# Attention and mixture of experts in one kernel: routing links moved apart, q and k loaded in halves, gathers dealt out one by one, and both ends of the attention re-ordered

## The chip, the core and the metric

The kernel runs on one core of a Trainium2 chip. The metric is the device time of one execution in microseconds (us). Five engines work side by side, each through its own queue in order: TensorE (PE; its weight loads are listed as PEld), VectorE (DVE), ScalarE (ACT), GpSimd (POOL) and SyncE (SP), which here only issues DMAs. ScalarE and GpSimd issue some DMAs too. SBUF is the working memory, PSUM the memory into which TensorE writes.

## The reference

Eight batches of eight heads, 576 tokens, head size 64. q and k are rotated (rotary embedding), attention follows, and its output is the input of a layer of eight experts, in which each token goes to one expert:

```python
q_rot, k_rot = rotate(q), rotate(k)              # [8, 8, 576, 64]
attn = softmax(q_rot @ k_rot^T / sqrt(64))
x = (attn @ v) as [4608 tokens, 512]
logits = x @ w_gate + modality_bias[modality_id]  # 8 experts
e = argmax(logits);  g = softmax(logits)[e]
out[token] = g * (relu(x @ w1[e]) @ w2[e])        # 512 -> 1024 -> 512
```

All in float32. The kernel reaches that precision in the products of scores and experts by splitting each operand into a high and a low half (H, L) and summing three products.

## The kernel before, in words

**Attention.** The 64 heads are 32 pairs (`NPAIR`), four to a batch. A pair's q and k come as one tile of two halves, `R[:, 0]` and `R[:, 1]` (the second is the first with its halves of the head size swapped, so that a rotation is a*cos + b*sin). `rope_` (L224) has five parts: 0 multiplies a by COS (L230), 1 multiplies b by SIN (L232), 2 adds them (L234), 3 copies the high half on ScalarE (L236, the helper's line L221), 4 subtracts to get the low half (L238). In the order below parts 0 to 4 are called T1, T2, R, HI, LO. For pairs 0 and 1 VectorE does parts 0, 1, 2 and 4, for all others GpSimd. Two buffers `R` live in the staging areas ST1 and ST2 of the expert weights, COS behind the one, SIN behind the other. `swap` (L240) copies the halves to the other 64 partitions by DMA, into `SW`. `load` (L138) brings q and k, `loadv` (L142) brings V in four DMAs.

Scores are made in nine units S0 to S8 (L250, matmuls L261) in a ring of three PSUM tiles. `rowmin` (MN, VectorE, L270) and `expo` (EX, ScalarE, L277) turn a unit into P; then `fill` (F0 to F3, FA, FB, L283) transposes P on TensorE, and ScalarE (A_) and VectorE (B_) evict the transposes into PH and PD. `AV` (AVA, AVB, L339) multiplies by V in two parts, `avout` (OT) copies to oT, `outp` (OUTA, OUTB, L370; the last rows in L373) turns the result with RW, an identity beside the gate's weights, so that x and its logits come in one product; `ev` (EVA, EVB, L384 to L390) scales by the reciprocal sums into X, into G (logits) and into XT (the last 64 tokens). `xout` (XO) stores a batch of X to DRAM in five DMAs.

**Order.** Nothing is scheduled by need: `J` (L700) gives each of these steps a key, a step of pair n stands at its key in `KEYS` plus n x 14.438 (`PER`), and all are issued in the order of keys (L819). The engines go through their queues in that order. So the keys, which are in the unit of microseconds of the plan, say what stands behind what; they start nothing at a time. `AT` holds the keys of routing and experts.

**Routing.** After the last pair of a batch `route` (L405) computes the token's expert and its rank among the expert's tokens, in 13 links that go from engine to engine (`rk` in `AT`): reductions on VectorE, comparisons on GpSimd, exponentials on ScalarE, one product on TensorE (L450, L452). They stand from 0 to 15.2 behind the pair's EVA, in the next pair. `scatter` (L469) writes five times to a table TAB in DRAM, by indirect DMA of GpSimd, one every 9 us of the plan. TAB holds, expert by expert, the token and its weight.

**Experts.** The tokens of an expert are taken in blocks of 256. `plan` (L479) computes the blocks: a first plan of `NA` = 8 whole blocks from the batches 0 to 5 (28 links from pair 23 on, on GpSimd and VectorE, 1.5 apart; among them a shift, L492), and a second one of up to 17 from all tokens, of which 11 are unrolled and six more stand in a guarded loop (L895), which runs when the second plan has over 11. A block: `m_ix` (L601) loads indices from TAB on SP's queue, `m_gather` (L608, L614) fetches rows of X into XG by eight indirect DMAs, `m_tr`/`m_tre` (L653, L657) transpose and split them, `m_l1` (L663, L673) is the first layer, `m_l1e` (L677) its relu and split, `m_l2` (L684, L690) the second layer, scaled into y (L693) and scattered to the output (L694). Weights come by `m_load1` and `m_load2` (L624, L629; left out where the expert stays), and `m_hi`, `m_lo` split them (L218, L221). Block 0 is placed by hand among the last pairs (L789 to L818): its plan and weights, gathers, splits and its first layer, whose four parts stand between AVB and OUTA of pair 31; the gathers of blocks 0, 1 and 2 are issued by turns. The attention's buffers are then released as a whole (L824), the two planes of W2 and y are allocated in their place, and a loop (`chain`, L845) goes on with the blocks. The last batch's routing, its scatters and the second plan are put between its steps.

**Start.** `setup` (L170) clears buffers and loads constants by DMAs of GpSimd; pair 0 is loaded and rotated in three chunks of columns (`FIRST`, L151), then pair 1 whole; `setup2` (L202) computes the modality's part of the logits and two constants, on GpSimd. The units of pair 0 stand in the order of all pairs, S8 first, which needs the last chunk.

Of the kernel before, what the change touches and what calls it, by code (L numbers as in the profile page):

```python
# [8 lines left out]
F32 = mybir.dt.float32  # L9
# [9 lines left out]
P = 128  # L19
# [6 lines left out]
NB_STATIC = 11  # L26
EMPTY = 1 << 20
# [17 lines left out]
    rk=(0, 0.6, 1.5, 4.7, 5.5, 6.3, 6.9, 7.5, 9.6, 10.4, 11.2, 14.4, 15.2),  # L45
    pl=1.5,
    sc=(10.5, 9.0),
    tr=3.5,
    te=-8.0,
    hi=(-14.0, -9.0, -5.0, -1.0),  # L50
    l1=(7.0, 10.0, 13.7, 17.6),
    l1e=3.0,
    sp2=(0.2, 0.4, 1.4, 1.8),
    l2=2.0,
    w1=(1.0, 5.7, 8.0, 10.2),
    w2=(-8.0, -5.0, -2.0, 1.0),
    plan=(-99.0, -15.0, 4.0, 6.0, 8.0, 10.0, 12.0, 14.0),
    ix=(-16.5, -9.5, 4.0, 6.0),
    rows=4.0,
    gap=1.3,  # L60
# [5 lines left out]
def tile_attention_moe(ctx: ExitStack, tc: tile.TileContext, qk, v, mod, wg, mb, w1, w2, rope, cf, ci, out):  # L66
# [42 lines left out]
    pp = att.enter_context(tc.tile_pool(name="pp", bufs=1))  # L109
# [4 lines left out]
    PJ = [pp.tile([P, 2 * S], F32, name=f"P{j}") for j in range(4)]  # L114
    P4 = pp.tile([P, S + 128], F32, name="P4")
    PH = pp.tile([P, 8, S], F32, name="PH")
    PD = pp.tile([P, S], F32, name="PD")
    Vs = [pp.tile([P, 2, 5, 64], F32, name=f"V{i}") for i in range(2)]

    RW = pp.tile([P, 4, 2, 72], F32, name="RW")  # L120

# [16 lines left out]
    def load(n):  # L138
        nc.sync.dma_start(out=Rs[n % 2], in_=qk[n])
        st[n] = dict(R=Rs[n % 2], HL=HL[n % 2], SW=SW[n % 2], V=Vs[n % 2])  # L140

    def loadv(n):  # L142
        b, hp = divmod(n, 4)
        V = Vs[n % 2]
        for hh in range(2):
            src = v[b, 2 * hp + hh]
            nc.sync.dma_start(out=V[:, hh, 0:4, :], in_=src[0:512, :].rearrange("(p j) d -> p j d", j=4))
            nc.sync.dma_start(out=V[hh * 64:hh * 64 + 64, hh, 4, :], in_=src[512:576, :])

# [7 lines left out]
    load(1)  # L157
# [10 lines left out]
    G = rc.tile([P, 5, 9, E], F32, name="G")  # L168

    def setup():  # L170
# [10 lines left out]
        for h in range(4):  # L181
            for s in range(2):
                g.tensor_copy(RW[s * 64:s * 64 + 64, h, s, 0:64], idf[s * 64:s * 64 + 64, s * 64:s * 64 + 64])
        g.memset(MI, 0)
        TI = PH.rearrange("p a b -> p (a b)")[:, 0:(E + 1) * N * 2 // P].bitcast(I32)
# [5 lines left out]
        for s in range(2):  # L191
            g.dma_start(out=RW[s * 64:s * 64 + 64, :, s, 64:72], in_=wg.rearrange("(c s d) e -> s d c e", s=2, d=64)[s])
        g.dma_start(out=CF, in_=cf)
        g.dma_start(out=VAL, in_=ci)
        m32 = mod.bitcast(I32).rearrange("(b s w) -> b s w", s=S, w=2)
        g.dma_start(out=MI[:, :, 0:4, :], in_=m32[:, 0:512, :].rearrange("b (p j) w -> p b j w", j=4))
        g.dma_start(out=MI[0:64, :, 4, :], in_=m32[:, 512:576, :].rearrange("b p w -> p b w"))
        for i in range(2):
            g.dma_start(out=MBB[:, i, :], in_=mb[i:i + 1, :].to_broadcast([P, E]))
        g.dma_start(out=TAB.rearrange("(p r) w -> p (r w)", p=P), in_=TI)  # L200

    def setup2():  # L202
        g = nc.gpsimd
        BT = PJ[0][:, 0:B * 5 * E].rearrange("p (b e) -> p b e", e=E)
        g.tensor_copy(MF, MI[:, :, :, 0])
        sh = [P, B * 5, E]
        mf = MF.rearrange("p b j -> p (b j)").unsqueeze(2).to_broadcast(sh)
        bi = BI.rearrange("p b j e -> p (b j) e")
        g.tensor_tensor(bi, mf, MBB[:, 1:2, :].to_broadcast(sh), op=ALU.mult)
        g.tensor_scalar(MF, MF, -1.0, 1.0, op0=ALU.mult, op1=ALU.add)  # L210
        g.tensor_tensor(BT, mf, MBB[:, 0:1, :].to_broadcast(sh), op=ALU.mult)
        g.tensor_tensor(bi, bi, BT, op=ALU.add)
        g.tensor_copy(UT, cview("U"))
        g.tensor_copy(RUN[:, 0, :], cview("EB"))
# [9 lines left out]
    def rope_(n, part, c0=0, c1=QW):  # L224
        d = st[n]
        e = nc.vector if n < 2 else nc.gpsimd
# [105 lines left out]
    def AV(n, half):  # L332
# [3 lines left out]
        for kt in range(5):  # L336
            for hh in range(2):
                r = PH[:, 4 * hh + kt, c0:c1] if kt < 4 else PD[:, c0:c1]
                nc.tensor.matmul(pa[hh * 64:hh * 64 + 64, 0:c1 - c0], d["V"][:, hh, kt, :], r, start=(kt == 0), stop=(kt == 4))  # L339
# [19 lines left out]
    def outp(n, half):  # L359
# [3 lines left out]
        if b not in bt_:  # L363
            bt_[b] = dict(x=xo.tile([P, 4, DM], F32, name="X", tag="X"), xt=xo.tile([P, 4, 72], F32, name="XT", tag="XT"))
        po = d["po", half] = psA.tile([P, 512], F32, name="pa", tag="pa")
        w = RW[:, hp].rearrange("p s c -> p (s c)")
        for i in range(2):
            for s in range(2):
                c = (2 * half + i) * P + s * 64
                nc.tensor.matmul(po[s * 64:s * 64 + 64, i * 144:i * 144 + 144], oT[:, c:c + 64], w, start=True, stop=True)  # L370
# [4 lines left out]
    def ev(n, half):  # L375
# [8 lines left out]
        nc.vector.tensor_tensor(xv, pv[:, :, 0:64].rearrange("p a (i f) -> p a i f", f=32),  # L384
                                rv.unsqueeze(2).unsqueeze(3).to_broadcast([P, 4, 2, 32]), op=ALU.mult)
        gv = G[:, j0:j0 + 2, 2 * hp:2 * hp + 2, :]
        nc.vector.tensor_tensor(gv, pv[:, :, 64:72].rearrange("p (j s) e -> p j s e", s=2),
                                rv.rearrange("p (j s) -> p j s", s=2).unsqueeze(3).to_broadcast([P, 2, 2, 8]), op=ALU.mult)
        if half:
            nc.vector.tensor_scalar(Bt["xt"][:, hp, :], po[:, 288:360], ri[:, 8:9], None, op0=ALU.mult)  # L390

    def xout(b):
# [3 lines left out]
        xt = xd[512:576, :].rearrange("p (i c f) -> p i c f", c=4, f=32)  # L396
        for i in range(4):
            s, o = i // 2 * 64, i % 2 * 32
            nc.sync.dma_start(out=xt[:, i], in_=Bt["xt"][s:s + 64, :, o:o + 32])
# [5 lines left out]
    def route(b):  # L405
        Bt = bt_[b]
        V_ = nc.vector
        G_ = nc.gpsimd
# [5 lines left out]
        for s in range(2):  # L414
# [583 lines left out]
```

## Time and profile before

| | |
|---|---|
| median of 3 runs | 983.05 us (978.0 to 984.02) |
| the profiled execution: its time, its span | 978.22 us, 976.4 us |
| TensorE busy | 908.2 us, 93% |
| VectorE, ScalarE, GpSimd busy | 674.2, 632.3, 663.8 us |
| mean granted TensorE clock | 0.982 |
| moved by DMA | 132.71 MB, mean 136 GB/s |

The profile is of one execution. The span goes from the first to the last instruction on the chip; the time holds what lies around it too. A line of the timeline gives start, duration, engine, line of the kernel, operation, what is written from what, and in brackets how long the engine stood idle before and who ended that. A line of the groups gives count, busy us and mean ns, then the idle time before and its causes. A line of the waits gives who waited for whom, us in total, how often, and the longest.

### The profile page before, as it was taken

Reading aid. Unit: us, or ns where it says so; the run is one execution under the profiler, and the core shown is the slowest. Engines: PE = TensorE matmul, PEld = TensorE weight load, DVE = VectorE, ACT = ScalarE, POOL = GpSimd, SP = SyncE. Lnnn points to the kernel's source line nnn. Section 1 sums busy time; section 2 is a strip of 40 time slices with the busy share of each in tenths; the row PEclk is TensorE's granted clock in tenths of the full one; section 3 lists DMA queues with packets and bytes.
Section 4 is the critical chain, followed back from the end, with each engine's and each line's share of the span. In section 5 each row is a group of like instructions: output and inputs, shape, how many; then the busy total and the mean of one; then the engine's idle time right before and its main releaser. Section 6 shows DMA issues by size and latency. Waiting matters only on the chain. (4 is left out here: it accounts for less than half of the span.)

```text
span 976.4 us, 24969 instructions
## 1 busy us (share of the span) xinstructions
PE 908.2 (93%) x9248; PEld 742.4 (76%) x9248; DVE 674.2 (69%) x1158; ACT 632.3 (65%) x1299; POOL 663.8 (68%) x498
## 2 busy tenths in 40 slices
PE   1899999999999999989977899999999999999996
PEld 1677677777777767767646689999998888899995
DVE  6677777787777777777754478677666666666771
ACT  1778787787787877868753355666555656556661
POOL 7776788889878798799656076557666666556500
PEclk9799999999999999999989899999999999999998
DMA  9645667566574755746751261111431611611100
GB/s 285 194 142 173 180 198 221 148 188 202 174 225 134 201 185 175 228 130 182 207 149 34 64 211 36 55 48 58 142 120 42 218 38 45 227 44 49 41 24 15
DMA packets 71964, 132.71 MB, mean 136 GB/s; under 512 B 28395, under 2 KB 48267, under 8 KB 66844
## 3 DMA queue, kind: packets, MB, share of 16 engines
q1 hardware_dynamic: 61436, 110.32, 37.8%
q0 software_dynamic: 9536, 19.48, 6.4%
q8 instruction: 75, 1.23, 0.6%
q10 hardware_dynamic: 864, 1.25, 0.4%
q14 instruction: 53, 0.43, 0.2%
HBM read 140.59 MB, written 19.77 MB: 164 GB/s over the span
## 5 line engine op out<-in xcount | busy, mean ns | idle before, releaser
L270 DVE TENSOR_REDUCE mn<-ps 128x1 f32<-128x576 f32 x288 | 205.4, 744 | 104.2 <-PE ps L261 67.3
L277 ACT ACTIVATE P<-ps,mn 128x576 f32<-128x576 f32 x288 | 210.4, 737 | 97.6 <-DVE mn L270 90.4
L614 POOL DMA_INDIRECT XG<-X,iy x152 | 180.9, 1190 | 47.5 <-issue 41.4
L673 PE MATMUL psH<-HL,W1H 128*128 128x256 f32 x1152 | 202.7, 279 | 0.0
L261 PE MATMUL ps<-HL 64*128 64x288 f32 x960 | 170.7, 315 | 29.8 <-ACT HL L221 14.9
L261 PE MATMUL ps<-SW 64*128 64x288 f32 x960 | 170.3, 316 | 9.0 <-DMA SW<-HL 4.7
L261 PEld LDWEIGHTS ps<-HL 64*128 64x128 f32 x960 | 137.7, 190 | 53.2 <-ACT P L277 15.9
L673 PEld LDWEIGHTS psH<-HL,W1H 128*128 128x128 f32 x1152 | 176.8, 188 | 1.7
L673 PE MATMUL psH<-HL,W1L 128*128 128x256 f32 x576 | 160.8, 279 | 0.7 <-DVE W1L L218 0.7
L261 PEld LDWEIGHTS ps<-SW 64*128 64x128 f32 x960 | 135.4, 190 | 24.4 <-ACT P L277 14.1
L218 DVE TENSOR_TENSOR W1L<-ST,W1H 128x1024 fp32r<-128x1024 f32 x76 | 90.0, 1222 | 84.6 <-ACT W1H L221 82.6
L339 PE MATMUL pa<-PH,V 128*64 128x320 f32 (+1 forms) x1024 | 142.2, 420 | 1.1 <-PE ps L261 0.7
L694 POOL DMA_INDIRECT out_dram<-y,ix x38 | 39.1, 1030 | 143.6 <-ACT y L693 129.8
L690 PE MATMUL psY<-W2H,SW 128*128 128x512 f32 x304 | 120.3, 396 | 1.4 <-ACT W2H L221 1.4
L690 PE MATMUL psY<-W2L,SW 128*128 128x512 f32 x304 | 120.4, 396 | 0.4 <-DVE W2L L218 0.4
L283 PE MATMUL ps<-idf,P 64*128 64x64 f32 x2624 | 105.3, 229 | 8.8 <-DVE PH L315 2.4
L283 PEld LDWEIGHTS ps<-idf,P 64*128 64x128 f32 x2624 | 92.6, 141 | 22.7 <-ACT PH L221 8.6
L315 DVE COPY PH<-ps 128x512 f32<-128x512 f32 (+1 forms) x160 | 97.3, 632 | 17.4 <-PE ps L283 10.9
L339 PEld LDWEIGHTS pa<-PH,V 128*64 128x64 f32 x1024 | 69.8, 139 | 51.5 <-issue 14.5
L673 PEld LDWEIGHTS psH<-HL,W1L 128*128 128x128 f32 x576 | 108.2, 188 | 0.9 <-DVE W1L L218 0.9
L221 ACT ACTIVATE PH<-ps 128x512 f32<-128x512 f32 (+1 forms) x160 | 84.0, 556 | 22.1 <-PE ps L283 14.9
L218 DVE TENSOR_TENSOR W2L<-ST,W2H 128x1024 fp32r<-128x1024 f32 x76 | 92.4, 1220 | 4.1 <-ACT W2H L221 3.6
(159 smaller groups left out, 1602.9 us busy)
## 6 DMA issues: line engine op xcount, KB each, us to landing
ST<-in_moe_w_dram SPq DMA_DIRECT2D x152, 512.0 KB
ST<-in_qk_dram SPq DMA_DIRECT2D x31, 1216.0 KB
SW<-HL SPq DMA_DIRECT2D x124, 232.0 KB
V<-in_v_dram SPq DMA_DIRECT2D x64, 128.0 KB
X<-X SPq DMA_DIRECT2D x8, 1024.0 KB
XG<-X,iy POOLq DMA_INDIRECT x152
V<-in_v_dram SPq DMA_DIRECT2D x64, 16.0 KB
X<-XT SPq DMA_DIRECT2D x32, 32.0 KB
```

The source lines that it names most:

```text
L218: nc.vector.tensor_tensor(o, a, b, op=ALU.subtract)
L221: return nc.scalar.activation(o, i, AF.Copy, scale=scale)
L261: free(nc.tensor.matmul(ps[:, g, 0:288], t[:, wq, q0:q0 + P], t[:, wk, k0:k0 + 288], start=(m == 0), stop=(m == len(L) - 1)), seen)
L270: lastmin[d["ring", u]] = nc.vector.tensor_reduce(mn, d["S", u][:, :, 0:288], op=ALU.min, axis=AX.XY).ins
L277: nc.scalar.activation(p.rearrange("p (a b) -> p a b", a=2), ps[:, :, 0:288], AF.Exp, bias=d.pop(("m", u)), scale=-1.0, accum_out=d["sum"] ...
L283: free(nc.tensor.transpose(ps[0][:, g, c:c + 64], src[r, k0:k0 + P], idf[r, r]), ps[1])
L315: mine.append((nc.vector.tensor_copy if g else acopy)(o, i).ins)
L339: nc.tensor.matmul(pa[hh * 64:hh * 64 + 64, 0:c1 - c0], d["V"][:, hh, kt, :], r, start=(kt == 0), stop=(kt == 4))
L614: nc.gpsimd.indirect_dma_start(out=XG[s % 2][:, t, g, :], out_offset=None, in_=X.rearrange("n (i f) -> (n i) f", f=P)[0:rows], in_offset=b ...
L673: nc.tensor.matmul(ps[:, i, :], w[:, c, f0:f0 + P], x[:, c, :], start=(m == 0), stop=(m == 11))
L690: nc.tensor.matmul(ps, hx[:, c, t * P:(t + 1) * P], w[:, c, :], start=(m == 0), stop=(m == 23))
L694: nc.gpsimd.indirect_dma_start(out=out, out_offset=bass.IndirectOffsetOnAxis(ap=d["ix"][:, t, 0:1], axis=0), in_=y, in_offset=None, bounds ...
```

## The change

- **Routing.** 15 links for 13 (the first copy goes to GpSimd as a step of its own, some are re-ordered), at keys from 23.0 to 73.3 behind the batch's last pair, so over three and a half pairs. Scatters stand one a pair from 73.4 on. In the last batch GpSimd's part goes to VectorE.
- **First plan.** It covers five batches (`NPL`), not six, begins after pair 19, has nine links (`plan0`), without the shift and the casts; whole blocks are counted by comparing with multiples of 256. Scatters of other batches are declared independent of each other, and those of batches 5 to 7 of block 0 to 7's index loads.
- **Loads.** `load` takes a half; b comes first, long ahead (key -48.9), a at -39.33 as before; b x SIN (now at T1) is done before a x COS. V comes in three DMAs, XT goes out in two, from two buffers; the gate's columns lie 4 by 4 behind 32 of x.
- **Gathers.** Each of the gathers of blocks 0, 1, 2 has a key, some wait for a named matmul (AV or OUT of pair 30, the first layer of block 0).
- **Start.** Pair 0's units get keys of their own (`first`), S1 and S0 ahead; pair 1 is rotated by GpSimd, but for its LO; constants are loaded by ScalarE's queue; `setup2` goes to VectorE in two parts, at 12.9 and 17.3 of pair 0.
- **End.** Pair 31 has keys of its own (`last`), both AV halves at once after the fills, then block 0's first layer, with the output products in it. W2's planes lie in the places of P and of PH, released one by one (`weights2`); W2 is split among the first layer's steps. y has its own pool from the start.

Core of the diff:

```diff
-    rk=(0, 0.6, 1.5, 4.7, 5.5, 6.3, 6.9, 7.5, 9.6, 10.4, 11.2, 14.4, 15.2),
-    pl=1.5,
-    sc=(10.5, 9.0),
...
+    rk=(23.0, 28.55, 31.2, 36.9, 41.45, 43.0, 44.4, 45.7, 54.6, 56.9, 57.4, 58.85, 60.2, 70.35, 73.3),
+    sc=(73.4, 87.85, 102.3, 116.7, 116.75),
+    pl=(58.9, 70.4, 73.35, 84.85, 87.75, 99.3, 102.2, 113.7, 116.6),
+    ix=(-41.5, -3.9, 6.1, 9.1),
+    sine=-48.9,
+    rows=(((0, -27.5, None), (1, -13.05, None), (2, -12.4, None), (3, -2.9, (30, "av", 0)), (5, 0.45, (30, "av", 1)),
+           (7, 4.75, (30, "out", 1))), ((0, 11.15, ("l1", 0)),), ((0, 16.5, None),)),
+    hi=(-14.8, -14.7, -0.4, -0.3),
+    lo=(-11.8, -1.6, 10.8, 10.85),
+    tr=(10.2, 10.21),
+    te=(10.3, 10.4),
+    hi2=(10.5, 10.98, 11.1, 11.2),
+    lo2=(11.5, 11.55, 11.65, 11.75),
+    last=dict(AVA=10.3, AVB=10.4, RE=10.2, RI=10.25, OTA=10.96, OTB=11.0, OUTB=11.2, OUTA=11.21, ...),
+    l1=(11.1, 11.3, 11.4, 11.42),
+    first=dict(S1=-5.9, S0=-5.85, MN1=-5.8, MN0=-5.75, EX1=-5.7, EX0=-5.65, S6=-5.55, S7=-5.5, ...),
+    second=dict(HI=-20.04, LO=-19.79),
+    consts=(12.9, 17.3),
...
-    def load(n):
-        nc.sync.dma_start(out=Rs[n % 2], in_=qk[n])
+    def load(n, half):
+        nc.sync.dma_start(out=Rs[n % 2][:, half], in_=qk[n, :, half])
...
-        e = nc.vector if n < 2 else nc.gpsimd
+        e = nc.vector if n == 0 or (n, part) == (1, 4) else nc.gpsimd
...
+    def weights2(i):
+        places[i].close()
+        W2[i] = ctx.enter_context(tc.tile_pool(name=f"w2{i}", bufs=1, reuse_waits="tile", ...)).tile(
+            [P, 8, DM], F32R, name="W2" + "HL"[i])
...
-    def setup2():
-        g = nc.gpsimd
+    def setup2(part):
+        g = nc.vector
...
+    def plan0():
+        G_ = nc.gpsimd
...
+        most = NPL * S // BLK
+        G_.tensor_tensor(nf, RUN[0:1, NPL, :], cview("EB")[0:1], op=ALU.subtract)
+        G_.tensor_scalar(th, sl[:, 0:most], float(BLK), float(BLK), op0=ALU.mult, op1=ALU.add)
+        G_.tensor_tensor(full, nf.unsqueeze(2).to_broadcast(sh), th.unsqueeze(1).to_broadcast(sh), op=ALU.subtract)
+        G_.tensor_scalar(full, full, 0.0, None, op0=ALU.is_ge)
+        yield
+        total(nb, full)
...
+        if after is not None:
+            tc.add_manual_dep(inst.ins, (l1_[after[1]] if after[0] == "l1" else st[after[0]][after[1:]]).name, ...)
...
-        if n > 1:
-            for part, nm in enumerate(("T1", "T2", "R", "HI", "LO")):
+        if n > 0:
+            for part, nm in ((1, "T1"), (0, "T2"), (2, "R"), (3, "HI"), (4, "LO")):
                 K_(nm, rope_, n, part)
...
-        if n > 3:
-            K_("LD", load, n)
+        if n > 2:
+            J(AT["sine3" if n == 3 else "sine"], "LD", n, load, n, 1)
+            K_("LD", load, n, 0)
```

422 lines of the change are left out of this document (246 added, 176 removed).

## The prediction, made before the changed kernel ran

> **What bounds the kernel now.** I read the page first, then TensorE's idle gaps in the timeline, and with them cut the span into five stretches and asked for the busy time of each.
>
> ```profile
> span 976.4 us, 24969 instructions
> PE 908.2 (93%) x9248; PEld 742.4 (76%) x9248; DVE 674.2 (69%) x1158; ACT 632.3 (65%) x1299; POOL 663.8 (68%) x498
> ```
> ```profile
> 14.86:47.24 32.38, 24.34 (x251) 18.90 (x252) 22.80 (x32) 18.20 (x45) 25.98 (x14) 0.84 0.68 213
> 47.24:473.64 426.40, 408.32 (x5697) 306.21 (x5695) 318.95 (x701) 329.21 (x869) 354.98 (x221) 1.00 0.62 182
> 473.64:563.99 90.35, 72.06 (x714) 53.56 (x711) 50.25 (x94) 45.43 (x97) 40.17 (x41) 0.91 0.38 104
> 563.99:967.58 403.59, 403.50 (x2596) 363.76 (x2596) 274.18 (x315) 235.87 (x286) 230.11 (x193) 1.00 0.26 85
> 967.58:976.40 8.82, 0.00 (x0) 0.00 (x0) 0.00 (x0) 0.69 (x1) 0.97 (x1) 0.70 0.06 21
> ```
>
> Columns of the second view: stretch, length, busy us (and instructions) of PE, PEld, DVE, ACT, POOL, granted clock, DMA share, GB/s. TensorE is the bound: 908.2 of 976.4 us. The cuts are events on it. 14.86 is the first score matmul. 47.24 and 473.64 are the second output projection (L373) of pair 0 and of pair 28; 563.99 is where TensorE has block 1 of the experts before it, 967.58 the last output.
>
> ```profile
> 14.86 0.60 PE L261 MATMUL ps<-HL 64*128 64x288 f32 x1 [14.86 <-ACT HL L221]
> ...
> 18.42 0.60 PE L261 MATMUL ps<-SW 64*128 64x288 f32 x1 [2.96 <-DMA SW<-HL]
> ...
> 32.08 4.13 PE L283 MATMUL ps<-idf,P 64*128 64x64 f32 x71 [0.44 <-ACT P L277]
> ...
> 47.24 0.29 PE L373 MATMUL pa<-RW,oT 128*64 128x72 f32 x4
> ...
> 473.64 0.29 PE L373 MATMUL pa<-RW,oT 128*64 128x72 f32 x4
> ```
>
> The experts' stretch is TensorE alone (403.50 of 403.59 us). Two outputs one block apart give its pace:
>
> ```profile
> 945.18 0.69 ACT L693 ACTIVATE y<-psY,ix 128x512 f32<-128x512 f32 x1 [3.02 <-issue]
> ...
> 967.58 0.69 ACT L693 ACTIVATE y<-psY,ix 128x512 f32<-128x512 f32 x1 [4.91 <-PE psY L690]
> ```
>
> That is 22.40 us a block, and 18 blocks are 403.2. Nothing in the change touches these matmuls, so 403.6 and the 8.8 of the tail stay. What can move is ahead of 563.99. For its floor I take a pair undisturbed by routing, and set beside it one with routing and the worst:
>
> ```profile
> 61.75:76.35 14.60, 14.44 (x206) 10.82 (x204) 10.89 (x24) 11.54 (x31) 11.09 (x4) 1.00 0.56 174
> ...
> 106.29:121.49 15.20, 14.53 (x213) 10.92 (x211) 11.28 (x27) 11.63 (x31) 11.85 (x10) 1.00 0.53 165
> ...
> 408.68:428.47 19.79, 16.07 (x212) 12.27 (x210) 15.10 (x30) 12.66 (x34) 16.19 (x17) 0.91 0.59 176
> ```
>
> A pair is 14.44 us of TensorE and takes 14.60 when clean. Pairs 0 to 28 are 28 intervals in 426.40, 15.23 each: 426.40 - 28 x 14.60 = 17.6 us lost. From 473.64 on the work left is three pairs and block 0: 3 x 14.44 + 22.40 = 65.7 of 90.35, 24.6 lost. At the start, pair 0 is 32.4 us on its way from the first matmul to 47.24.
>
> **The change, part by part: pairs 0 to 28.** What delays a pair here is mostly GpSimd, which rotates q and k:
>
> ```profile
> POOL ST L230 <- DMA ST<-in_qk_dram: 51.1, 25, 3.9
> ```
> ```profile
> L238 POOL TENSOR_TENSOR HL<-ST,HL 128x1216 fp32r<-128x1216 f32 x28 | 77.8, 2780 | 3.8 <-ACT HL L221 3.7
> ```
>
> Four instructions of 2.78 us make a pair 11.1 us of GpSimd; the stretch's 354.98 busy us are 12.7 a pair, with scatters and routing. To that come 51.1 / 28 = 1.8 us a pair in which it waits for a q, k load. The sum, 14.5, is a pair's whole 14.6, so whatever GpSimd must wait for in a routed batch (for a reduction of VectorE, say) becomes lateness of the next rotation. The half loads take the 1.8 away: the second half is asked for at -48.9 in place of -39.33 and used first (T1 at -32.78), the first is used at -26.38; 13 to 16 us replace 6.5. They are two issues on SP where there was one (about 0.6 us more a pair there; the merged V load takes one back). With 12.7 of 14.6 us GpSimd then has 1.9 us spare. The routing's links stand 0.5 to 10.2 us apart, over 50 us of the order, where they stood 0.6 to 3.2 apart over 15, so an engine that comes to its link finds the one before it done.
>
> The 19.79 is one event:
>
> ```profile
> 420.67 2.75 POOL L238 TENSOR_TENSOR HL<-ST,HL 128x1216 fp32r<-128x1216 f32 x1
> 420.72 2.72 DVE L492 TENSOR_SCALAR ni<-ni 1x8 int32<-1x8 int32 x1 [0.76 <-POOL ni L490]
> ...
> 425.08 0.60 PE L261 MATMUL ps<-HL 64*128 64x288 f32 x1 [2.75 <-ACT P L277]
> ```
> ```profile
> 425.08:428.50 3.42, 3.42 (x28) 3.13 (x30) 2.22 (x4) 3.14 (x9) 3.42 (x3) 0.52 0.99 316
> ```
>
> An 8-element shift held VectorE for 2.72 us, until GpSimd's rotation ended; the minima behind it came late, TensorE stood 2.75 us, and then ran 3.42 us at a clock of 0.52. The pair lost 19.79 - 14.60 = 5.2. The new first plan has no such shift and 9 steps for 28, so this goes whatever else happens. The routing's own matmuls stay (x213 for x206, 14.53 for 14.44). I take 14.70 a pair: 28 x 14.70 = 411.6, a gain of 14.8. Ends: only the 5.2, and all 17.6. If the spread cover fails, each routed pair keeps its 0.6.
>
> **From pair 28 to block 1.** Now the stalls are these:
>
> ```profile
> SPq L604 <- DMA TAB<-VAL,oi: 55.7, 4, 23.6
> ```
> ```profile
> 502.44 0.58 PE L261 MATMUL ps<-HL 64*128 64x288 f32 x1 [2.38 <-DVE XG L655]
> ...
> 516.07 0.40 PE L261 MATMUL ps<-HL 64*128 64x288 f32 x1 [4.03 <-ACT P L277]
> ```
> ```profile
> 532.20:548.20 16.00, 12.15 (x70) 8.42 (x68) 2.15 (x4) 1.91 (x4) 4.98 (x5) 0.79 0.13 17
> ```
> ```profile
> L673 PE MATMUL ps<-HL,W1H 128*128 128x256 f32 x64 | 12.3, 288 | 2.6 <-issue 2.6
> ```
>
> SP's queue waits for scatters ahead of its index loads, with swaps and V loads behind them; VectorE and ScalarE sit at XG's transpose, waiting for gathers, with minima and exponentials of pairs 30 and 31 queued behind (2.38 and 4.03 us of TensorE, each with a clock drop); and block 0's first layer is issued with holes (a wait for nothing that shows). After: the plan covers five batches and its last step stands 22 us earlier, the scatters of later batches are declared independent, and block 0's gathers run from -27.5 to 4.8 of pair 31 while its transposes stand at 10.2, behind every score and fill of that pair. Nothing of the last two pairs queues behind XG any more.
>
> ```profile
> L339 PE MATMUL pa<-PH,V 128*64 128x320 f32 (+1 forms) x1024 | 142.2, 420 | 1.1 <-PE ps L261 0.7 <-issue 0.4
> ...
> L221 ACT ACTIVATE W1H<-ST 128x1024 fp32r<-128x1024 f32 x76 | 76.2, 1051 | 0.0
> ...
> L221 ACT ACTIVATE HL<-XG 128x512 fp32r<-128x512 f32 x38 | 39.8, 1141 | 28.1 <-DVE XG L655 11.1 <-DVE HX L682 7.1 <-issue 4.1
> ```
>
> The first layer starts after both AV halves of pair 31 (142.2 / 32 = 4.4 us of TensorE at least), time in which ScalarE does two splits of 1.14 us, VectorE two transposes and two subtractions. The W2 planes lie where P and PH were, so W2 is split under the first layer and not after it. What I keep as loss over 65.7: 1.2 us for the last fill's eviction (no scores are left to cover it), 0.15 x 3, 1.2 for the W1 halves on ScalarE (two of 1.05 us in each of the last two pairs, before exponentials), and 2.0 for issue holes, since block 1's gathers again run beside the first layer. Together 70.5, a gain of 19.8. Ends: 66.8 (gain 23.5), and 81 (gain 9) if one XG wait and its clock drop stay.
>
> **The start.** Rows of VectorE and GpSimd in pair 0 and 1:
>
> ```profile
> 12.72 0.69 DVE L232 TENSOR_TENSOR ST<-ST,ST 128x512 f32<-128x512 f32 x1 [1.63 <-DMA ST<-in_rope_dram]
> ...
> 15.45 1.42 DVE L230 TENSOR_TENSOR ST<-ST,ST 128x1216 f32<-128x1216 f32 x1
> ...
> 17.04 1.78 POOL L209 TENSOR_TENSOR BI<-MF,MBB 128x320 f32<-128x320 f32 x1
> ...
> 18.26 1.84 DVE L234 TENSOR_TENSOR ST<-ST 128x1216 f32<-128x1216 f32 x1
> ...
> 23.16 2.07 DVE L270 TENSOR_REDUCE mn<-ps 128x1 f32<-128x576 f32 x3
> ...
> 38.39 2.78 POOL L238 TENSOR_TENSOR HL<-ST,HL 128x1216 fp32r<-128x1216 f32 x1 [3.86 <-ACT HL L221]
> ...
> 41.95 1.42 DVE L270 TENSOR_REDUCE mn<-ps 128x1 f32<-128x576 f32 x2 [2.24 <-PE ps L261]
> ```
>
> For the change: the first minimum waits until 23.16 only because VectorE rotates pair 1 first. Given to GpSimd (3 x 2.78 = 8.3 us), that time is free, and S1 and S0, put first, need only the first two of the three chunks. At best the first fill starts at 27 in place of 32.08, and 13.8 us later (13.2 between their keys and some loss) comes the projection, at 40.8: gain 6.4. Against it: both engines on SBUF exclude each other here. VectorE's 1.42 us instruction took 1.84 when GpSimd's L209 (to 18.82) was under way, as the shift did above. GpSimd's first rotation can start when the tables land, 12.72, just when VectorE still has three instructions of pair 0's last chunk; behind two rotations of 2.78 they come 4 to 5 us late, and eat the gain. And the routing constants move from GpSimd to VectorE as seven instructions at 12.9 and 17.3 of pair 0, in idle gaps such as the 2.24 us before 41.95. There GpSimd has LO, T2, R and T1 in a row from 38.39: if each small instruction lets one rotation pass, VectorE is held up to 11.1 us, 8.9 beyond the gap. I bound this at nothing and 8 us, and take 3, the shift's 2.72. The start in sum: 1 us lost, ends -6.4 and +8.
>
> By the Trainium skill ("GPSIMD Engine Reference", Key points) GpSimd shares its SBUF interfaces with VectorE and contends with instructions that read two SBUF inputs or run in a two-port mode. The trace agrees (2.72 and 1.84 us); it says nothing of who goes first. Taken as every such instruction waiting out a rotation, it would put the start at +8 and the time at 951.5.
>
> **At nothing:** fewer X, V and token-tail DMAs, two buffers for the token tails, the last batch's routing on VectorE, and one expert change more lie beside the experts' 403.50 busy TensorE us or beside SP's idle time; uncovered, the load would cost at most a block, 22.4.
>
> **Sum.** 976.4 + 1.0 - 14.8 - 19.8 = 942.8 span. The profiled execution took 978.22, 1.8 beyond its span: 944.6. The runs' median, 983.05, is 4.8 above that; the range covers it.
>
> **Rivals.**
> (a) The start gains too: GpSimd gets its data late enough to let VectorE through; 944.6 - 7.4 - 4 (fewer issue holes and W1 delays) = 933. For it: the 7.7 us of VectorE set free. Against: the two held instructions.
> (b) GpSimd stays late: the wait for loads goes, but waits for ScalarE's HI (3.8 us so far) and reductions grow, or the constants cost all their 8. Half the steady gain and 7 more at the start: 959.
> (c) The change doesn't do what it says: the waits land on other pairs and at other links; 5.2 of the steady loss and 5 of the transition go: 976.4 + 1 - 10.2 + 1.8 = 969.
> (d) Slower, by one mechanism: the first plan's eight slots are whole blocks of five batches, no longer six. If these hold fewer than eight, a slot is wasted, the second plan needs a twelfth block, and the guarded loop for six more runs: 6 x 22.4 = 134, about 1079. The profile's gathers
>
> ```profile
> L614 POOL DMA_INDIRECT XG<-X,iy x152 | 180.9, 1190 | 47.5 <-issue 41.4
> ```
>
> are 152 = 19 x 8, so today it is exactly 8 + 11. It decides at eight; the reference's inputs give 2 + 5 + 2 = 9 whole blocks in 2880 tokens, which speaks against it.
>
> **How the numbers follow.** Forecast 0.50 (944.6; its own range 936 to 954), (a) 0.20, (b) 0.21, (c) 0.06, (d) 0.02, 0.01 unnamed. All best ends give 931, all worst 972. Range 929 to 966: it leaves (d), the worse part of (c) and the best corner out. One per cent is about what a measurement of this kernel tells from no change: faster by more 0.93 (all of the first three and half of (c)), within it 0.04, slower 0.03.
>
> **Right or wrong.** Right: 28 intervals of L373 near 14.7; no VectorE instruction of the plan above 0.5 us; GpSimd's wait for q, k loads under 10 us; 68 to 73 us from pair 28 to block 1; the stretch after it unchanged at 403.6. Wrong: a first projection past 52 or before 42; gaps over 2 us beside XG; more than 152 gathers.

## The result, and the profile after

| | before | after |
|---|---|---|
| median of 6 runs, us | 983.51 (978.0 to 993.7) | 950.43 (948.56 to 952.82) |
| profiled execution / its span, us | 978.22 / 976.4 | 950.52 / 948.7 |
| ratio to before, 95% interval | | 0.9681 (0.9654 to 0.9708) |

The kernel became 3.2% faster; 944.6 had been forecast, 936 to 954 as the forecast's own range. Ratios here and below compare fast runs with fast runs (the 993.7 of before is a slow one), so they differ a little from quotients of the medians. The page of the profile after, to be held against the two lines of before: TensorE does the same 9248 matmuls in less span.

```profile
span 948.7 us, 24948 instructions
...
PE 901.9 (95%) x9248; PEld 740.3 (78%) x9248; DVE 677.6 (71%) x1170; ACT 630.0 (66%) x1292; POOL 663.0 (70%) x485
```

Cut at the same five events (the second output projection is L421 here), with the same columns: length, busy us of PE, PEld, DVE, ACT, POOL, granted clock, DMA share, GB/s.

```profile
14.09:54.27 40.18, 26.61 (x252) 20.68 (x253) 29.01 (x36) 19.70 (x48) 31.62 (x12) 0.96 0.74 209
54.27:464.76 410.49, 405.44 (x5695) 304.06 (x5695) 315.29 (x697) 326.19 (x858) 352.67 (x224) 1.00 0.69 187
464.76:537.06 72.30, 65.73 (x715) 51.45 (x711) 49.85 (x97) 45.80 (x101) 31.67 (x33) 0.98 0.41 116
537.06:941.66 404.60, 404.17 (x2596) 364.09 (x2596) 275.48 (x323) 235.36 (x285) 240.10 (x197) 1.00 0.30 97
941.66:948.70 7.04, 0.00 (x0) 0.00 (x0) 0.00 (x0) 0.69 (x1) 0.97 (x1) 0.74 0.08 27
```

| stretch | before | forecast | after | after less forecast |
|---|---|---|---|---|
| to pair 0's projection | 47.24 | 48.24 | 54.27 | +6.0 |
| pairs 0 to 28 | 426.40 | 411.6 | 410.49 | -1.1 |
| pair 28 to block 1 | 90.35 | 70.5 | 72.30 | +1.8 |
| experts and tail | 412.41 | 412.4 | 411.64 | -0.8 |
| span | 976.4 | 942.8 | 948.7 | +5.9 |

So 33.96 us came out of two stretches, and the start gave 7.0 back where 1.0 had been allowed. In pairs 0 to 28 TensorE is idle for 5 of 410 us; the wait of GpSimd for a q, k load no longer appears, and what is left of its waits is this one (us in total, times, longest), which an engine with time to spare has:

```profile
POOL HL L284 <- ACT HL L267: 39.8, 23, 5.7
```

The start is read from TensorE's timeline; the brackets are idle time just before the row and what ended it.

```profile
22.12 0.61 PE L307 MATMUL ps<-SW 64*128 64x288 f32 x1 [4.97 <-DMA SW<-HL]
...
31.21 0.60 PE L307 MATMUL ps<-SW 64*128 64x288 f32 x1 [2.89 <-ACT P L323]
...
50.82 0.61 PE L307 MATMUL ps<-HL 64*128 64x288 f32 x1 [4.08 <-ACT P L323]
...
54.27 0.23 PE L421 MATMUL pa<-RW,oT 128*64 128x72 f32 x2
```

Three gaps. The exponential named at the last one waited for a minimum, and the minimum stood behind three routing constants (L252 to L254) on VectorE. VectorE's rows, then GpSimd's:

```profile
26.23 3.40 DVE L284 TENSOR_TENSOR HL<-ST,HL 128x1216 fp32r<-128x1216 f32 x1
...
41.28 1.54 DVE L252 CAST MF<-MI 128x40 f32<-128x40 int32 x1
42.85 3.02 DVE L253 TENSOR_TENSOR BI<-MF,MBB 128x320 f32<-128x320 f32 x1
45.90 2.61 DVE L254 TENSOR_SCALAR MF<-MF 128x40 f32<-128x40 f32 x1
48.43 1.41 DVE L316 TENSOR_REDUCE mn<-ps 128x1 f32<-128x576 f32 x2
...
50.49 0.47 DVE L257 TENSOR_TENSOR BT<-MF,MBB 128x320 f32<-128x320 f32 x1
```
```profile
25.57 2.77 POOL L276 TENSOR_TENSOR ST<-ST 128x1216 f32<-128x1216 f32 x1 [0.22 <-DVE mn L316]
28.42 3.82 POOL L280 TENSOR_TENSOR ST<-ST 128x1216 f32<-128x1216 f32 x1
...
40.00 2.78 POOL L284 TENSOR_TENSOR HL<-ST,HL 128x1216 fp32r<-128x1216 f32 x1 [5.02 <-ACT HL L267]
42.73 2.78 POOL L276 TENSOR_TENSOR ST<-ST,ST 128x1216 f32<-128x1216 f32 x1
45.59 2.88 POOL L280 TENSOR_TENSOR ST<-ST 128x1216 f32<-128x1216 f32 x1
```

Read them as pairs: L252 ends at 42.82, where GpSimd's L284 ends (42.78); L253 at 45.87, just past the end of L276 (45.51); L254 at 48.51, where L280 ends (48.47). Each small instruction is held until one rotation of GpSimd is over, the next rotation slips in, and the next small one is held again: 7.2 us for three. L257, with L253's 320 elements, takes 0.47 when GpSimd is idle. The hold goes both ways: VectorE's subtraction at 26.23 waits for L276 to end at 28.34, and L280 then takes 3.82 in place of 2.78. After the 4.08 us gap TensorE also ran slowly (clock 0.51, so about half of these 3.45 us is lost):

```profile
50.82:54.27 3.45, 3.45 (x28) 3.16 (x29) 3.08 (x7) 3.18 (x9) 2.71 (x2) 0.51 0.26 106
```

### The profile page after: what moved, and what is told of

Same layout as the page of the kernel before. It is cut to its first block, busy times and chain, and to the rows that moved or that the text cites. A ratio compares the mean times of both kernels' runs of the same rounds, so it can differ in the third digit from the quotient of the medians.

```text
span 948.7 us, 24948 instructions
## 1 busy us (share of the span) xinstructions
PE 901.9 (95%) x9248; PEld 740.3 (78%) x9248; DVE 677.6 (71%) x1170; ACT 630.0 (66%) x1292; POOL 663.0 (70%) x485
## 5 line engine op out<-in xcount | busy, mean ns | idle before, releaser
L729 POOL DMA_INDIRECT XG<-X,iy x152 | 185.9, 1223 | 71.6 <-issue 54.5
L307 PE MATMUL ps<-SW 64*128 64x288 f32 x960 | 167.7, 315 | 23.2 <-DMA SW<-HL 20.2
L307 PE MATMUL ps<-HL 64*128 64x288 f32 x960 | 167.5, 313 | 4.4 <-ACT P L323 4.4
L385 PE MATMUL pa<-PH,V 128*64 128x320 f32 (+1 forms) x1024 | 138.3, 412 | 2.7 <-ACT oT L267 1.4
L815 POOL DMA_INDIRECT out_dram<-y,ix x38 | 40.3, 1060 | 129.4 <-ACT y L814 107.7
L284 POOL TENSOR_TENSOR HL<-ST,HL 128x1216 fp32r<-128x1216 f32 x30 | 83.3, 2777 | 45.1 <-ACT HL L267 45.0
```

The lines of the kernel that those rows point to most:

```text
L284: e.tensor_tensor(d["HL"][:, 1, c], a, d["HL"][:, 0, c].bitcast(F32), op=ALU.subtract)
L307: free(nc.tensor.matmul(ps[:, g, 0:288], t[:, wq, q0:q0 + P], t[:, wk, k0:k0 + 288], start=(m == 0), stop=(m == len(L) - 1)), seen)
L385: i = nc.tensor.matmul(pa[hh * 64:hh * 64 + 64, 0:c1 - c0], d["V"][:, hh, kt, :], r, start=(kt == 0), stop=(kt == 4))
L729: inst = nc.gpsimd.indirect_dma_start(out=XG[s % 2][:, t, g, :], out_offset=None, in_=X.rearrange("n (i f) -> (n i) f", f=P)[0:rows], in_o ...
L815: nc.gpsimd.indirect_dma_start(out=out, out_offset=bass.IndirectOffsetOnAxis(ap=d["ix"][:, t, 0:1], axis=0), in_=y, in_offset=None, bounds ...
```

## The experiments

Twelve kernels, in three groups of four, each group on a chip of its own. Each ratio is to the kernel before on the same chip (its medians there: 974.28, 977.76 and 984.70 us), so times are compared across groups by ratio alone. The three stretches are read from one profiled execution of each kernel. "Start" counts from the first score matmul to pair 0's projection, since the first matmul itself lies between 13.1 and 15.3 us in kernels whose code for it is the same. Six executions with nearly one and the same code of the start (the changed kernel, its repeat, and four whose edit lies later; of these whole_loads, the 37.9, also has pair 4's two half loads joined within the start) give 37.9 to 40.3 there; a difference inside that spread is no finding.

| kernel | median us | ratio (95%) | start | pairs 0 to 28 | 28 to block 1 |
|---|---|---|---|---|---|
| before | 983.51 | 1 | 32.4 | 426.4 | 90.4 |
| after | 950.43 | 0.9681 (0.9654 to 0.9708) | 40.2 | 410.5 | 72.3 |
| consts_gpsimd | 939.85 | 0.9622 (0.9582 to 0.9662) | 34.5 | 410.8 | 68.2 |
| swap_before_load | 942.33 | 0.9661 (0.9631 to 0.9691) | 36.7 | 410.4 | 67.8 |
| lo1_gpsimd | 942.02 | 0.9662 (0.9628 to 0.9696) | 38.0 | 411.1 | 67.5 |
| pair1_vector | 946.26 | 0.9691 (0.9654 to 0.9729) | 40.0 | 411.3 | 68.4 |
| whole_loads | 972.49 | 0.9946 (0.9918 to 0.9973) | 37.9 | 437.6 | 67.6 |
| close_routing | 955.11 | 0.9760 (0.9727 to 0.9793) | 39.8 | 417.2 | 70.8 |
| small_copies | 950.98 | 0.9729 (0.9691 to 0.9768) | 38.5 | 411.7 | 67.8 |
| gathers1_early | 945.45 | 0.9661 (0.9620 to 0.9702) | 40.3 | 411.2 | 68.0 |
| control_after | 953.56 | 0.9672 (0.9624 to 0.9720) | 39.9 | 411.8 | 75.4 |
| three_edits | 943.99 | 0.9587 (0.9541 to 0.9632) | 32.9 | 410.8 | 73.9 |
| three_and_ota | 942.27 | 0.9574 (0.9527 to 0.9622) | 30.7 | 411.5 | 73.4 |
| before_halves | 992.20 | 1.0065 (1.0030 to 1.0100) | 32.4 | 422.3 | not read |

**The constants (consts_gpsimd).** In `setup2`:

```diff
-        g = nc.vector
+        g = nc.gpsimd
```

> The seven routing constants go back to GpSimd, at the same two keys of pair 0; all else as in the changed kernel (950.4 us; pair 0's last projection at 54.3 us). Port theory: the three instructions that held VectorE from 41.28 to 48.51 are gone, with them TensorE's gap of 4.08 us and 3.4 us at half clock; GpSimd does them in its idle time before HI of pair 2. First projection near 48.5, time near 944.5. Rival (the gap comes from late data of pair 1, the swaps behind a load): the gap stays within 1 us of where it was and the time stays at 949 to 952.

Pair 0's projection came at 48.37 in place of 54.27, 5.9 us earlier (from the first matmul 5.7; 3.4 to 5.8 against the six executions), and the gap of 4.08 us, which stands with 4.08 to 4.11 in every one of the six executions with the unchanged start, is gone. That gap and half of the 3.45 us at the lower clock make 5.8. On GpSimd the same three instructions cost 1.2 us in all:

```profile
35.11 0.21 POOL L252 CAST MF<-MI 128x40 f32<-128x40 int32 x1
35.40 0.74 POOL L253 TENSOR_TENSOR BI<-MF,MBB 128x320 f32<-128x320 f32 x1
36.23 0.23 POOL L254 TENSOR_SCALAR MF<-MF 128x40 f32<-128x40 f32 x1
```

So the 7.2 us on VectorE were not its own work, and they were on the path of the start. In the ratios the intervals of this kernel and of the changed one still touch; it is the vanished gap that shows it.

**The swap behind a load (swap_before_load).** The first half load of pair 2 moved behind pair 0's last swap in SP's order:

```diff
-            elif part == 2 and i == 2:
-                load(2, 1)
...
+    load(2, 1)
     load(2, 0)
```

> Pair 2's first half load is issued behind the swaps of pair 0's last chunk instead of ahead of them. Rival theory (the start is lost to the swap that lands late, TensorE idle 4.97 us until 22.12): the third score unit starts near 19, and 3 us come through to the end, about 947.5. Port theory: the gap of 4.97 shrinks by 2 to 3 us, but VectorE is still held by LO of pair 1 until GpSimd's rotation is through, so the next gap (2.89 us) takes it up again: time 949 to 951.

The gap ahead of pair 0's last chunk fell from 4.97 us (4.6 to 6.1 in the six executions) to 2.16, but a second one of 1.86 (1.16 in the changed kernel) came behind it, and the constants' gap stayed (3.95). The start from the first matmul is 36.7, 1.3 below the six executions' lowest: a gain of one to three us.

```profile
20.04 0.60 PE L307 MATMUL ps<-SW 64*128 64x288 f32 x1 [2.16 <-DMA SW<-HL]
...
22.50 0.60 PE L307 MATMUL ps<-SW 64*128 64x288 f32 x1 [1.86 <-DMA SW<-HL]
...
48.01 0.40 PE L307 MATMUL ps<-HL 64*128 64x288 f32 x1 [3.95 <-ACT P L323]
```

**Pair 1's low half (lo1_gpsimd)** and **all of pair 1 (pair1_vector).** In `rope_`, the two edits in turn:

```diff
-        e = nc.vector if n == 0 or (n, part) == (1, 4) else nc.gpsimd
+        e = nc.vector if n == 0 else nc.gpsimd
```

> The low half of pair 1 (one instruction) goes from VectorE to GpSimd too. Port theory: VectorE is no longer held 3.40 us from 26.23 on, so the minima behind it and the exponentials come 2 to 3 us earlier, and the gap of 2.89 us at 31.21 goes, with some of the cold clock; GpSimd has 5 us of idle time before HI of pair 2 for it. Time near 947.5. Rival: no change, 949 to 951, since TensorE then waits for pair 1's swap.

```diff
-        e = nc.vector if n == 0 or (n, part) == (1, 4) else nc.gpsimd
+        e = nc.vector if n < 2 else nc.gpsimd
```

> Pair 1 is rotated by VectorE again, whole, ahead of pair 0's first minima, as in the kernel before; the other parts of the start stay. If giving it to GpSimd was a gain, this is 2 to 5 us slower than 950.4. Port theory: the engines no longer cross in the first 20 us (VectorE's subtraction of chunk three starts 1.1 us earlier, LO is not held), but the first minimum waits again until 21 to 23; about even, 948 to 952.

With the low half on GpSimd the gap of 2.89 us at 31.21 went (it is 0.9 to 3.4 in the six executions), and the last gap grew from 4.08 to 4.82: GpSimd, busier by 2.78 us, meets the constants all the same. The start, 38.0, is inside the spread, so a gain by itself isn't shown.

```profile
48.02 0.60 PE L307 MATMUL ps<-HL 64*128 64x288 f32 x1 [4.82 <-ACT P L323]
```

With pair 1 back on VectorE the start is 40.0, and all three gaps stand (5.05, 3.35, 4.09): giving the rotation to GpSimd neither gained nor lost by itself. The time set free on VectorE was no time that TensorE waited for.

**All three together (three_edits)** on the changed kernel, with **the control** in the same group:

> The changed kernel once more, unchanged, as the yardstick for the other three on the same chip. If the start of 54.3 us, the 410.5 us of pairs 0 to 28 and the 72.3 us of the transition belong to the kernel, the same stretches come out within 0.7 us of these. If the about 4 us of issue holes near 520 us belonged to that one execution, the transition is 67.5 to 68.5 us, as in the experiments so far, and the profiled execution is 943.5 to 945.5 us.

> The seven routing constants on GpSimd, the swap of chunk 3 ahead of the first half load, and the low half of pair 1 on GpSimd, all three together. If they lie one behind another on the path of the start, their gains add: 5.9 + 2.8 + 2.8 = 11.5 us, so that pair 0's second output projection is at 42.8 us and the time is 11 to 12 us below the control's. Rival: they cut the same wait twice, and GpSimd, which now has all of pair 1 and the constants, is late for pair 1's swaps: the projection at 45 to 48 us, the first interval after it 15 us or more, the time 6 to 8 us below the control's.

The control's start and pairs agree with the first profile (39.9 and 411.8; the pairs differ by 1.3), its stretch from pair 28 doesn't: 75.4 (more on it below). The three edits lowered the median by 9.6 us against the control; the intervals 0.9541 to 0.9632 and 0.9624 to 0.9720 overlap by a hair. Counted from the first matmul the start is 32.9, and 30.7 in the last kernel, whose start has the same code: 31.8 in the mean, against 39.9, a gain of 8.1. The projections, at 48.19 and 45.42, are about where the rival had them (45 to 48, the sum 42.8); the median's 9.6 lies between the two. No gap of TensorE for an exponential is over 0.3 us in this profile; what remains are swaps:

```profile
23.08 0.60 PE L307 MATMUL ps<-SW 64*128 64x288 f32 x1 [3.34 <-DMA SW<-HL]
...
38.06 0.40 PE L307 MATMUL ps<-SW 64*128 64x288 f32 x1 [1.56 <-DMA SW<-HL]
```

The second is pair 1's swap, 1.56 us late: the rival's effect, though the pair after it took 14.58. In this execution the experts took 407.4 us, and in that of the small copies 409.0, where all others took 403.6 to 404.6; nothing in either edit reaches that stretch. The 407.4 has three holes of TensorE without a named cause (0.33, 0.45 and 0.26 us, from 560 on) and then 3.5 us at a clock of 0.53, as in the last stretch below; in the 409.0 TensorE was busy for 408.95, and why isn't settled.

**Half loads undone (whole_loads).** From pair 4 on, one load as before, at its old place:

```diff
-            J(AT["sine3" if n == 3 else "sine"], "LD", n, load, n, 1)
-            K_("LD", load, n, 0)
+            if n == 3:
+                J(AT["sine3"], "LD", n, load, n, 1)
+                K_("LD", load, n, 0)
+            else:
+                K_("LD", load, n, slice(0, 2))
```

> From pair 4 on q and k come in one load again, at the key of the second half. Prediction's theory: GpSimd waits for loads again, up to 1.8 us a pair, and with it busy 12.6 of 14.66 us the routed pairs get late: 28 intervals grow from 410.5 to 413 to 418, time 953 to 958. Rival (the close routing alone made the pairs slow): the wait shows on GpSimd, but the intervals stay at 410.5 to 412, time 950 to 952.

Pairs 0 to 28 grew by 27 us, to 437.6, past even the kernel before (426.4). GpSimd's waits in that stretch, its rows, and TensorE's:

```profile
POOL ST L278 <- DMA ST<-in_qk_dram: 53.7, 21, 5.8
```
```profile
290.33 2.80 POOL L278 TENSOR_TENSOR ST<-ST 128x1216 f32<-128x1216 f32 x1 [5.79 <-DMA ST<-in_qk_dram]
```
```profile
301.96 0.60 PE L307 MATMUL ps<-SW 64*128 64x288 f32 x1 [3.17 <-DMA SW<-HL]
```

The wait for loads is back at its old size (51.1 before), but single waits are longer (5.8 for 3.9), and this order of steps doesn't cover them: four of the pairs take 18.2 to 20.2 us, and the pairs as a whole are slower than either forecast (413 to 418, or 410.5 to 412). Why the same total costs more here than before was not taken apart. An argument, not a test: the whole load needs the buffer that LO frees two pairs earlier, so a late LO makes the next load late, and that the next LO; a half load asked for earlier cuts this ring.

**Half loads alone (before_halves).** The kernel before, with:

```diff
+            J(-48.9, "LD", n, load, n, 1)
-            K_("LD", load, n)
+            K_("LD", load, n, 0)
...
-            for part, nm in enumerate(("T1", "T2", "R", "HI", "LO")):
+            for part, nm in ((1, "T1"), (0, "T2"), (2, "R"), (3, "HI"), (4, "LO")):
```

> The kernel before, with the half loads of q and k alone (the sine half early, the two products in the other order); routing, gathers, start and last outputs as before. If the late load is what lengthened its pairs, the wait of GpSimd for it falls from 51 us to under 15, pairs 0 to 28 take about 417 us instead of 426.4, and the time falls by 9 us, to a ratio near 0.991. Rival: that wait was hidden in the kernel before, whose pairs were lengthened by the routing's steps standing close together, and the whole loads hurt only where the first instruction waits for both halves: pairs 0 to 28 then take 424 to 427 us and the ratio is 0.998 to 1.002.

Here the last pair's cosine product comes after the experts' first weights have taken the cosines' place, so it multiplies by those and waits for them; the time past pair 28 is not read, and the ratio says nothing about the half loads. Pairs 0 to 28 took 422.34, 4.1 less than before. The wait for loads is gone, but other waits of GpSimd took its place. The wait of the routing for VectorE, first in the kernel before, whose GpSimd waited for loads, then here, with the wait for HI:

```profile
POOL dl L423 <- DVE mx L420: 4.7, 3, 2.8
...
POOL dl L423 <- DVE mx L420: 27.5, 7, 5.9
POOL HL L238 <- ACT HL L221: 24.5, 13, 3.6
```

And nearly all of the 4.1 us is one event: the shift that VectorE was held on for 2.72 us in the kernel before met the end of a rotation of GpSimd (it ends at 421.23),

```profile
420.40 0.86 DVE L492 TENSOR_SCALAR ni<-ni 1x8 int32<-1x8 int32 x1
```

and the pair of 19.79 us did not occur (the longest is 16.0). Routed pairs still take 15.2. The 422.3 lies between the two forecasts (417, and 424 to 427); without the one event it would be the rival's. So the rival holds for this part: the wait for loads was hidden in the kernel before.

**Routing close together (close_routing).** The fifteen routing steps within 15 us of the order in place of 50, half loads kept:

```diff
-    rk=(23.0, 28.55, 31.2, 36.9, 41.45, 43.0, 44.4, 45.7, 54.6, 56.9, 57.4, 58.85, 60.2, 70.35, 73.3),
+    rk=(25.53, 25.83, 26.13, 27.03, 30.23, 31.03, 31.83, 32.43, 35.13, 35.93, 36.53, 36.73, 37.43, 39.93, 40.73),
```

> The routing's 15 links stand as close as before (25.5 to 40.7 behind the pair instead of 23.0 to 73.3); plan and scatters stay where the change put them. Prediction's theory: the half loads leave GpSimd enough spare time, so only part comes back, 0.2 us a pair in routed batches: intervals 412 to 416, time 952 to 956. Rival (the links' waits for each other are the cost): nearly all of the 12 us that the spread gained beside the plan comes back, intervals near 420, time near 960.

Pairs 0 to 28 took 417.2, 6.7 more and between the two forecasts (412 to 416, and 420); the ratio, 0.9760, lies clear above the changed kernel's. GpSimd now waits in the routing for a reduction of VectorE, as in the half loads alone, and in the last stretch TensorE stood 3.31 us for the routing's one-hot rows:

```profile
POOL dl L479 <- DVE mx L476: 27.2, 7, 5.5
```
```profile
475.01 0.18 PE L501 MATMUL pa<-OH,UT 128*128 128x48 bf16 x1 [3.31 <-POOL OH L493]
```

**Who is held (small_copies).** Inside undisturbed pairs, VectorE was given extra small instructions on 1x8 elements that nothing reads: one copy in pairs 8 and 9, three in 10 and 11, one and three reductions in 16 to 19.

```diff
+            if copy:
+                nc.vector.tensor_copy(t, cview("SL")[0:1, 0:8])
+            else:
+                nc.vector.tensor_reduce(t[:, 0:1], cview("SL")[0:1, 0:8], op=ALU.add, axis=AX.X)
```

> Extra work, results unused: at the constants' key, in VectorE's idle gap, one copy of 8 elements in pairs 8 and 9, three in pairs 10 and 11, one sum of 8 elements in pairs 16 and 17, three in 18 and 19. Port theory: each copy waits for GpSimd's rotation (up to 2.8 us), three in a row let two more pass (up to 8 us), the sums take 0.2 us each; pairs 8 and 9 lose 0 to 3 us, 10 and 11 lose 4 to 8 each, 16 to 19 nothing; time 958 to 970. Rival (what held VectorE at the start was something of the start): no copy above 0.3 us, time 950 to 952.

VectorE's rows for a copy and a reduction, and then what GpSimd was doing at these times:

```profile
161.93 1.09 DVE L267 COPY pb<-CF 1x8 f32<-1x8 f32 x1
...
176.62 0.98 DVE L267 COPY pb<-CF 1x8 f32<-1x8 f32 x1
191.11 1.24 DVE L267 COPY pb<-CF 1x8 f32<-1x8 f32 x3
...
279.77 0.14 DVE L269 TENSOR_REDUCE pb<-CF 1x1 f32<-1x8 f32 x1
```
```profile
160.22 2.77 POOL L292 TENSOR_TENSOR HL<-ST,HL 128x1216 fp32r<-128x1216 f32 x1 [1.45 <-ACT HL L275]
...
174.81 2.78 POOL L292 TENSOR_TENSOR HL<-ST,HL 128x1216 fp32r<-128x1216 f32 x1 [1.06 <-ACT HL L275]
...
278.06 2.78 POOL L292 TENSOR_TENSOR HL<-ST,HL 128x1216 fp32r<-128x1216 f32 x1 [1.43 <-ACT HL L275]
```

The copies end at 163.02 and 177.60, where GpSimd's subtractions end (162.99 and 177.59). The reduction ran its 0.14 us in the middle of one. So it is the kind of instruction that is held, and for whatever is left of GpSimd's. Three copies in a row were held once, not three times: at 191.11 they took 1.24 us together, and GpSimd, done at 192.18, had no further rotation ready. So the 4 to 8 us expected for each of these pairs did not come; that fits a new hold only where GpSimd has its next long one ready, as at the start. The four pairs with copies took 14.58 to 14.83 us, as without: a hold of 1 us in steady pairs is covered.

**The last stretch (gathers1_early, three_and_ota).** Block 1's first gathers from behind the first layer to behind pair 30's output, and, on the three edits, ScalarE's copy of the last attention output ahead of the W2 splits:

```diff
-           (7, 4.75, (30, "out", 1))), ((0, 11.15, ("l1", 0)),), ((0, 16.5, None),)),
+           (7, 4.75, (30, "out", 1))), ((0, 4.95, (30, "out", 1)),), ((0, 16.5, None),)),
```

> Block 1's eight gathers stand right behind block 0's, beside the last pair's fills and AV, not beside block 0's first layer. If gathers make TensorE's issue holes (five of 0.28 to 0.44 us from 519.5 on): the holes go from the first layer, about 2 us from pair 28 to block 1 (72.3 to 70.5), time near 949, or show up at the fills instead. If not: the holes stay where they are, 72.3 stays.

```diff
-    last=dict(..., OTA=10.96, ...
+    last=dict(..., OTA=10.45, ...
```

> The three edits, and of the last pair's first half the copy of the attention output ahead of the splits of W2 on ScalarE instead of behind them. If TensorE's 1.45 us before the second half's attention product are a wait for that copy, the stretch from pair 28 to block 1 of the experts is 66.1 us instead of 67.6, and the time 1.3 us below that of the three edits. Rival: ScalarE now waits for the first half's product with the splits queued behind it, and the split weights are late by as much: the stretch is 67.5 us or more and the time the same.

Neither decides. In the changed kernel's first layer of block 0 the profile shows holes in which TensorE waited for nothing that it can name, 1.1 + 0.7 us from 519.5 on, none longer than 0.44, and right behind them the clock falls. A matmul of the layer takes 0.28 us up to there and about 0.41 in this window, so the mean of the 96 is 0.295; with early gathers there are neither holes nor fall, and the mean is 0.28:

```profile
521.90:525.35 3.45, 3.12 (x13) 2.85 (x13) 0.17 (x1) 0.60 (x1) 0.00 (x0) 0.51 0.08 24
```
```profile
L794 PE MATMUL ps<-HL,W1H 128*128 128x256 f32 x64 | 12.6, 296 | 1.2 <-issue 1.1 <-DVE HX L803 0.2
L794 PE MATMUL ps<-HL,W1L 128*128 128x256 f32 x32 | 9.4, 295 | 0.7 <-issue 0.7
```
```profile
L794 PE MATMUL ps<-HL,W1H 128*128 128x256 f32 x64 | 11.5, 282 | 0.2 <-DVE HX L803 0.2
L794 PE MATMUL ps<-HL,W1L 128*128 128x256 f32 x32 | 8.9, 279 | 0.0
```

But all eight kernels of the first two groups are without the holes, with the gathers at either place, and the stretch is 67.5 to 68.4 in seven of them; the control and the two kernels with the three edits, in the third group, have them again. In the control the clock then stays at 0.51 for 6.8 us, which is part of why its stretch is 75.4. They go with the chip or the execution, and what makes them is open. In three_and_ota the wait for the copy fell from 1.45 us to 0.54,

```profile
497.22 2.37 PE L385 MATMUL pa<-PH,V 128*64 128x320 f32 x16 [0.54 <-ACT oT L267]
```

while the stretch fell by only 0.5 and the median by 1.7, well inside the intervals. Its 0.9574 is the best ratio of the study.

## Why the prediction was right, and where it was not

**The sum held because its two large terms did, the second in part by luck.** Pairs 0 to 28: 14.70 a pair was forecast, 410.49 / 28 = 14.66 came. Pair 28 to block 1: 70.5 forecast, 72.30 came. Of what was kept as loss there, the last fill's eviction is 1.28 us (1.2 taken) and the issue holes 1.8 (2.0 taken); the copy of the attention output behind the W2 splits, 1.45 us, had been missed, as had the 3.45 us at a clock of 0.51 behind the holes.

That TensorE was busy for 65.73 of the 72.30 us, and 65.7 had been counted as work, is luck: 65.73 holds the time at the lower clock. In the seven experiments without holes or a fall of the clock the same matmuls took 62.8 to 63.1 us, for instance in consts_gpsimd:

```profile
459.20:527.38 68.18, 63.07 (x715) 49.81 (x711) 49.96 (x97) 45.75 (x101) 32.29 (x33) 1.00 0.45 123
```

So the work was counted about 2.7 us too high (for one, pair 31's own stretch has 170 matmuls and 12.75 us there, not 206 and 14.44), and the losses of the first profile were about 9.3 us, not the 4.85 forecast; in those seven they were 4.7 to 5.3. Nothing over 2 us stands beside XG, the plan's reductions on VectorE take 0.2 us, the gathers are 152, and the experts took 404.6, 1.0 more than said. Of the rivals, (d) did not happen; (a)'s earlier start and (c)'s waits on other pairs did not come; (b)'s late start came, and its waits for HI grew (3.7 to 39.8 us), without (b)'s loss in the pairs.

**The step that failed is the start:** "I bound this at nothing and 8 us, and take 3, the shift's 2.72. The start in sum: 1 us lost". It is lost by 7.0 (54.27 for 47.24), beyond the 52 that was named as the sign of an error. The mechanism was named (one rotation passes for each small instruction), its size was taken at one hold. It was three holds in a row, the gap behind them and a lower clock after it, and undoing them gave 5.9. The other part of that term failed too: less the constants the start was to gain 2 us and lost 1. The gain had rested on VectorE's time set free; handing pair 1 back to VectorE changed nothing (40.0 against 40.2). What the sum had left out stood on SP: a half load issued ahead of pair 0's last swap, 1 to 3 us.

By the Trainium skill ("GPSIMD Engine Reference", Key points) GpSimd contends with VectorE instructions that run in a two-port mode or read two SBUF inputs; by "VectorE: DVE Perf Modes", Mode 2x_2P, an fp32 copy takes both read ports. The runs agree with both: the one-input copy was held until 163.02, the reduction was not (0.14 us). Taken as the prediction noted it, every such instruction waiting out a rotation, the rule gave 951.5; the profiled execution took 950.52. The rule was nearer than the 2.72 us of a single row.

**Pairs 0 to 28 gained what was forecast, but not as told.** The working laid the routed pairs' lateness on GpSimd's 1.8 us a pair of waiting for loads, with the far-apart steps beside it. Alone, the half loads took that wait away and gave back 4.1 us, nearly all from the one event of 5.2 us; the far-apart steps without the half loads gave pairs 27 us longer than with them, and 11 longer than before; with both, 15.9 came off. The far-apart steps are worth 6.7 us by close_routing. So the two parts lean on each other: steps at fixed far places serve only an engine that is on time, and an engine on time serves only if the routing's links do not make it wait for VectorE (27 us in each of the two kernels with close steps and half loads, 4.7 in the kernel before). How much of the rest belongs to the shorter first plan was not tried.

## What to carry to other kernels

Before moving small work from GpSimd to VectorE, look at what GpSimd does at that moment: each instruction of the held kind costs up to one of GpSimd's if GpSimd has long ones ready in a row, so count the instructions, not their elements, and ask which minimum or eviction is queued behind them. Two edits that each look like the cause of a gain may be worth little alone, or harm: undo each in the new kernel and add each to the old one before a gain is laid to either. And compare one stretch over several executions before a difference of 2 or 3 us in it is believed.

## What the runs showed of the hardware that was not expected

- A hold between VectorE and GpSimd doesn't depend on size: 8 elements were held for 1.09 us and 40 for 2.61, in each case to the end of GpSimd's instruction; and GpSimd is held as well (3.82 us for 2.78).
- The held and the free instructions differ by kind: a copy, a cast, a shift and a product were held, a reduction was not.
- A gap of 4.08 us dropped TensorE's clock to 0.51 for the next 3.45 us. No gap of that length is needed: in the first layer of block 0, holes of 0.28 to 0.44 us in a row did the same (0.51 for 3.45 us from 521.90).
- In the start the clock column can't be read. It gives 1.00 up to the gap at 50.82, but until 33.3 us a score matmul takes 0.44 us, as it does behind that gap at 0.51; from 38 us on it takes 0.29:

```profile
24.52 0.44 PE L307 MATMUL ps<-HL 64*128 64x288 f32 x1
...
38.24 0.29 PE L307 MATMUL ps<-HL 64*128 64x288 f32 x1
...
51.22 0.44 PE L307 MATMUL ps<-HL 64*128 64x288 f32 x1
```
